# Loads of w_in by even and odd partitions, the first chunk's work regrouped, and two query blocks in buffers of their own

## The chip, the cores and the metric

The kernel runs on one core of a Trainium2 chip. The metric is the time of one execution on the device in microseconds (us). The core has a matrix engine (PE; its weight loads are shown apart as PEld), a vector engine (DVE), a scalar engine (ACT), a general engine (POOL, GpSimd) and a queue engine (SP) that issues most of the loads. SBUF is the on-chip memory of 128 partitions; PSUM is where PE writes, eight banks of 512 float32 a partition.

## The reference

Cosformer attention over 8 batches of 8 heads, 576 positions, head size 64, then a feed-forward layer over all 4608 tokens (512 to 2048 to 512):

```python
r = np.maximum(x, 0.0)                              # x is q or k
phi = np.concatenate([r * c, r * s], axis=-1)       # c, s: cos and sin of the position
kv = np.einsum('bhsf,bhsd->bhfd', k_p, v)
z = np.sum(k_p, axis=2)
num = np.einsum('bhsf,bhfd->bhsd', q_p, kv)
den = np.einsum('bhsf,bhf->bhs', q_p, z)[..., None] + 1e-06
attn = num / den                                    # tokens x 512: head * 64 + d
h = attn @ w_in
out = (h * (1.0 / (1.0 + np.exp(-beta * h)))) @ w_out
```

## The kernel before

**Tiling.** A batch is nine blocks n of 64 query positions. The feed-forward layer takes 512 tokens (eight blocks) at a time; that is a chunk, nine in all, so chunk 0 holds blocks 0 to 7 of batch 0, chunk 1 block 8 of batch 0 and blocks 0 to 6 of batch 1, chunk 2 blocks 7 and 8 of batch 1 and six of batch 2. Blocks 7 and 8 of batch 1 are thus wanted only by chunk 2.

**Attention of one batch.** load_raw (L76) brings q, k and v from DRAM into one buffer each (raw_q, raw_k, raw_v), which the next batch uses again. q_relu and k_relu (L195, L199) clip them into qb and rk (bf16), v_scale (L202) writes v times cosine and v times sine into vb, the first as nine DVE instructions of a block each, the second shared with ACT. q_turn_pe (L227) or q_turn_dma (L258) transposes qb into qt; tan_mul (L222) multiplies that by the tangent into qs. kv_mm (L270) builds kv; num_mm (L290) multiplies qt and qs with it; x_rden and x_mul (L303, L315) divide into xs, one of whose rows is two heads side by side; x_turn_pe or x_turn_dma (L351, L365) transposes xs into xt, the input of the layer. A DMA transpose is issued on SP like a load.

**The layer.** h_mm and h_act (L380, L391) are the first matmul and its activation for one of 16 groups jt of hidden units; o_part and o_mm (L553, L539) the second matmul of chunk 0. From chunk 1 on the second matmul has seven block products instead of eight (o_fast, L556), from chunk 3 on the first as well; these want sums on DVE: g_sum (L397) writes S1 to S4 from the activations, w_sums (L874) T1 to T4 from w_out, wh_sum (L436) those of w_in. In o_fast the product "1" goes to a bank, ACT copies it away ("c1", L602), and "6" adds to that same bank and reads S2; "a7" (DVE, L608) takes the bank before product "4" goes into it.

**Weights.** w_in comes as four stages of 1 MB (load_w, L95), one buffer w_stage each, and is cast to bf16 into win[i] (cast_win, L105); w_out takes the same four buffers after it (cast_out, L117). A stage holds w_in's rows in their order and win[i] holds them with the heads regrouped, so a cast goes in pieces of 64 partitions (GJ, L126).

**Order.** The program is written out by hand, engine by engine in the order of the calls. Up to L746 stands the start with batch 0 and stage 0 of w_in. Then comes a loop of 32 slots (L854): slots 0 to 15 are chunk 0's first matmul, 16 to 23 its second by quarters, 24 to 31 by one jt each for all four token tiles. The dictionary early (L807) hangs batch 1 onto slots: the eighth block of batch 0 and the list rest (L761, casts of w_in, the loads of batch 1 and w_out) after slot 4, kv of batch 1 after slot 22, its query transposes after 23 (second), its num after 25 and 26, x_turn_pe after 28 and 29. Batch 2 is loaded at slot 24 (L868). Then the 16 groups of chunk 1 (L882): num_rest, the last two blocks of batch 1, and att_q(2), the queries of batch 2, stand after group 0, k_all(2) after group 4, w_sums after 6, kv_all(2) and the tan_mul of batch 2 after 10; behind the loop q_relu(3) and the second matmul of chunk 1 (L911). Chunks 2 to 8 follow from lists (L938).

Each DMA issued on SP takes one of eight semaphores in turn and waits for the one eight issues before it.

Of the kernel before, what the change touches and what calls it, by code (L numbers as in the profile page):

```python
# [22 lines left out]
def kernel(  # L23
# [52 lines left out]
    def load_raw(b, name, j0=0, j1=4):  # L76
        js = slice(j0, j1)
        src = {"q": q, "k": k, "v": v}[name][b]
        nc.sync.dma_start(  # L79
            out=raw_tile(b, name)[:, js].rearrange("q j n d -> q j (n d)"),  # L80
            in_=src.rearrange("(j g) (p n) d -> (g p) j (n d)", g=2, n=NQ)[:, js, :])
# [8 lines left out]
    S1, S2, S3, S4 = (const.tile([P, JT // 2, TCH // 2], BF16, name=f"S{i}") for i in (1, 2, 3, 4))  # L90
    w_in_v = moe_w_in.rearrange("(j p) f -> p j f", p=P)
# [3 lines left out]
    def load_w(kind, i, step=4):  # L95
        if (kind, i) not in stages:
            stages[kind, i] = stage.tile([P, 4, 512], FP32, name="w_stage", tag="w_stage")
        st = stages[kind, i]
        for a in range(0, 4, step):
            if kind == "out":  # L100
                nc.sync.dma_start(out=st[:, a : a + step], in_=w_out_v[:, 4 * i + a : 4 * i + a + step, :])
                continue
            nc.sync.dma_start(out=st[:, a : a + step], in_=w_in_v[:, a : a + step, i * 512 : (i + 1) * 512])

    def cast_win(i, gj, eng="dve", f0=0, f1=512, jps=slice(0, 2)):  # L105

        g, jj = gj
        o = win[i].rearrange("q (jp g) f -> q jp g f", g=2)[jj * HP : (jj + 1) * HP, jps, g, f0:f1]
        a = stages["in", i].rearrange("q (jp jj) f -> q jp jj f", jj=2)[g * HP : (g + 1) * HP, jps, jj, f0:f1]
        if eng == "act":  # L110
            nc.scalar.copy(o, a)
        elif eng == "pool":
            nc.gpsimd.tensor_copy(o, a)
        else:
            nc.vector.tensor_copy(o, a)
# [10 lines left out]
    GJ = [(0, 0), (0, 1), (1, 0), (1, 1)]  # L126

    load_raw(0, "q", 0, 2)
    load_raw(0, "q", 2, 4)
    beta16 = const.tile([JT, P], FP32, name="beta16")  # L130
    nc.scalar.dma_start(out=beta16, in_=moe_beta.rearrange("(j p) -> j p", p=P))
# [63 lines left out]
    def q_relu(b, jp, eng="dve", n0=0, n1=NQ):  # L195
        return relu(qb[:, jp, n0:n1].rearrange("q n (j d) -> q j n d", j=2),
                    raw_tile(b, "q")[:, 2 * jp : 2 * jp + 2, n0:n1], eng)

    def k_relu(b, j0=0, j1=4, eng="dve", n0=0, n1=NQ):  # L199
        relu(rk.rearrange("q n j d -> q j n d")[:, j0:j1, n0:n1], raw_tile(b, "k")[:, j0:j1, n0:n1], eng)  # L200

    def v_scale(b, cs, jp=None, n0=0, n1=NQ, eng="dve"):  # L202
        t = (cos9, sin9)[cs]
        rv = raw_tile(b, "v")
        js = slice(0, 4) if jp is None else slice(2 * jp, 2 * jp + 2)
# [21 lines left out]
    def q_turn_pe(b, jp, bank, hold=False):  # L227

        parts = ((0, 0, 5), (1, 5, NQ))
        v2 = []  # L230
        for i, n0, n1 in parts:
            t = ps[:, bank + i].bitcast(BF16)[:, 0 : (n1 - n0) * P].rearrange("q (n c) -> q n c", c=P)
            v2.append(t)
            for n in range(n0, n1):
                nc.tensor.matmul(t[:, n - n0, :], lhsT=qb[:, jp, n, :], rhs=ident,
                                 is_transpose=True, start=(n == n0), stop=(n == n1 - 1))
        def take(e, i):
            _, n0, n1 = parts[i]
            if e == "act":
                nc.scalar.copy(qts[b % 2][:, jp, n0:n1], v2[i])  # L240
            else:
                tan_mul(nc.vector, qs_first[:, jp, n0:n1], v2[i], n0, n1)

        if hold:
            return take
        for e, i in (("act", 0), ("dve", 1), ("act", 1), ("dve", 0)):
            take(e, i)
# [22 lines left out]
    def kv_mm(b, jp, bank, jjs=(0, 1)):  # L270
        t = kv_out(jp, bank)
        for n in range(NQ):
            for jj in jjs:
                for g in range(2):
                    hs = slice(g * HP, (g + 1) * HP)
                    nc.tensor.matmul(  # L276
                        t[jj * HP : (jj + 1) * HP, g], lhsT=rk[hs, n, 2 * jp + jj, :],
                        rhs=vb[hs, n, 2 * jp + jj].rearrange("q s e -> q (s e)"),
# [10 lines left out]

    def num_mm(b, n, jp, bank, slot):  # L290

        for cs in range(2):
            for jj in range(2):
                rows = slice(jj * HP, (jj + 1) * HP)
                for g in range(2):
# [3 lines left out]
                        lhsT=(qts[b % 2], qs_of(b))[cs][rows, jp, n, cols],  # L299
# [15 lines left out]
    def x_mul(got, n0, n1):  # L315
        nv, rden, first, jps = got
        a, z, w = n0 - first, n1 - first, len(jps)
        o = xs[:, n0:n1, jps[0] : jps[-1] + 1].rearrange("q n s (j d) -> q j n s d", j=2)
# [6 lines left out]
    def x_mul_act(got, n):  # L325
        nv, rden, first, jps = got
        for s_, jp in enumerate(jps):
            for jj in range(2):
                nc.scalar.activation(xs[:, n, jp, jj * D : (jj + 1) * D], nv[:, jj, n - first, s_, 0:D],
# [355 lines left out]
    warm_pe(58, 48)  # L685
# [7 lines left out]
    for bank, n0, n1 in ((6, 0, 5), (7, 5, NQ)):  # L693
        nc.vector.tensor_copy(tanr[:, n0:n1, :].rearrange("q n p -> q (n p)"), ps[:, bank, 0 : (n1 - n0) * HP])
# [47 lines left out]
    for gj, eng in zip(GJ, ("pool", "dve", "pool", "dve")):  # L742
        cast_win(0, gj, eng, jps=slice(0, 1))
    for gj, eng in zip(GJ, ("act", "pool", "pool", "pool")):
        cast_win(0, gj, eng, jps=slice(1, 2))
# [10 lines left out]
    def cast_halves(i, fs=(0, 256)):  # L756
        for f in fs:
            for gj in GJ:
                cast_win(i, gj, "pool" if i > 1 and gj == GJ[3] else "dve", f, f + 256)

    cast_halves(1)  # L761

    def rest():

        cast_halves(2)
        cast_halves(3)
        x_mul(x_rden(2, 0, 8, NQ, (0, 1)), 8, NQ)
# [4 lines left out]
        load_raw(1, "q")  # L772
        load_w("out", 2, 2)
        load_w("out", 3, 2)
        x_turn_dma(0, 8, 9)
# [5 lines left out]
        q_relu(1, 0)  # L781
        q_relu(1, 1, n1=5)
# [6 lines left out]
    takes = []  # L789

    def second():

        takes.append(q_turn_pe(1, 0, 4, hold=True))
        takes.append(q_turn_pe(1, 1, 6, hold=True))
        cast_out(8)
        takes[0]("act", 0)
        takes[0]("dve", 1)
        cast_out(9, "a")
        takes[0]("dve", 0)
        takes[0]("act", 1)  # L800
        cast_out(10)
        for e, i in (("act", 0), ("dve", 1), ("act", 1), ("dve", 0)):
            takes[1](e, i)
        for j in (11, 12, 14, 15):
            cast_out(j, "a")

    early = {  # L807
        4: lambda: (num_mm(0, 8, 0, 2, 0), num_mm(0, 8, 1, 2, 1), rest()),
        15: lambda: (v_scale(1, 1, n1=8, eng="act"), k_relu(1, 2, 4, "act")),
        22: lambda: (kv_mm(1, 0, 6), kv_mm(1, 1, 6), kv_take((0, 1), 6, "act"), q_relu(1, 1, "act", 5)),  # L810
        23: second,
        25: lambda: (num_seven(0, 4), x_mul(x_rden(4, 0, 0, 7, (0,)), 0, 7), cast_out(13)),
        26: lambda: (num_seven(1, 6), x_mul(x_rden(6, 0, 0, 7, (1,)), 0, 7)),
        28: lambda: x_turn_pe(1, 0, 7, 4, ("act",), (0,)),
        29: lambda: x_turn_pe(1, 0, 7, 5, ("dve",), (1,)),
    }

    def num_rest():
        for n in range(7, NQ):
            for jp in range(2):  # L820
                num_mm(1, n, jp, 2, 2 * (n - 7) + jp)
        x_mul(x_rden(2, 0, 7, NQ, (0, 1)), 7, NQ)
# [31 lines left out]
    for slot in range(32):  # L854
# [13 lines left out]
        if slot == 24:  # L868
            for name in "qvk":
                load_raw(2, name)  # L870
# [10 lines left out]
    wx_tiles()  # L881
    for slot in range(16):  # L882
        h_group(1, slot)
        if slot == 0:
            num_rest()
# [9 lines left out]
        elif slot == 10:  # L895
            kv_all(2, eng="act")
            for jp in range(2):
                tan_mul(nc.vector, qs_of(2)[:, jp], qts[0][:, jp], 0, NQ)
    q_relu(3, 0, "act")
    q_relu(3, 1, "act")  # L900
    q_turn_dma(3)

# [11 lines left out]
    ops(y, "1 c1")  # L914
    for t, bank in enumerate((4, 6, 0)):
# [176 lines left out]
```

## Time and profile before

| | us |
|---|---|
| three runs: median (lowest to highest) | 274.01 (273.54 to 274.51) |
| the profiled execution: its own time | 274.44 |
| its span in the profile | 272.7 |
| PE busy | 265.3 (97%) |
| DVE busy | 224.0 (82%) |
| ACT busy | 188.4 (69%) |
| POOL busy | 68.3 (25%) |
| mean granted PE clock (1.00 is full) | 0.998 |

PE is busy 3.94 us of the first 5, then 5.00, 3.64 and 4.81 of the next three times 5, all of 20 to 60, 9.18 of 60 to 70, 9.85 of 70 to 80, and all but 0.07 of 80 to 230 (the table of busy time by stretch). Part of the first 17 us is matmuls on zeros that only keep PE running (warm_pe, warm_long).

The chain that ended last is read from the end backwards: at each step it goes to what released that step. A busy share alone says little here; what a step is worth is seen from which of two waits ends later at its place.

### The profile page before, as it was taken

The numbers are of one execution on the slowest core, as the hardware profiler recorded it, in microseconds if no ns is written. First come the engines' busy times: TensorE is split into PE (matmuls) and PEld (weight loads), VectorE is DVE, ScalarE is ACT, GpSimd is POOL, SyncE is SP. The second block draws the span as 40 slices with busy tenths as digits, with TensorE's granted clock in tenths as the row PEclk, the third lists the DMA queues.
The fourth block names the chain that finished last, engine by engine and source line by source line (L and its number), as shares of the span: only waits on it lengthen the run. The fifth ranks groups of instructions, "written<-read, shape, count | busy, mean of one in ns | idle before, by whom it ended". The sixth has DMA issues, their size and how long they took to land.

```text
span 272.7 us, 8970 instructions
## 1 busy us (share of the span) xinstructions
PE 265.3 (97%) x3712; PEld 206.8 (76%) x3712; DVE 224.0 (82%) x596; ACT 188.4 (69%) x384; POOL 68.3 (25%) x89
## 2 busy tenths in 40 slices
PE   8899999999899999999999999999999999999994
PEld 8554455455784588888888888888888888888883
DVE  5989969499989889789989997899589768757852
ACT  4778777796419656899489966996696179428920
POOL 1444000510078000660085009300840060000001
PEclk9999999999999999999999999999999999999999
DMA  6999999999969999994589439943600570015005
GB/s 237 374 395 383 392 390 319 379 201 336 284 130 311 240 348 226 240 313 103 147 216 370 92 58 223 332 71 62 181 2 2 61 185 1 2 27 130 0 2 155
DMA packets 50681, 54.00 MB, mean 198 GB/s; under 512 B 31232, under 2 KB 31760, under 8 KB 50640
## 3 DMA queue, kind: packets, MB, share of 16 engines
q1 hardware_dynamic: 47504, 45.55, 59.1%
q0 software_dynamic: 2784, 7.61, 9.6%
q8 instruction: 29, 0.48, 0.7%
q10 hardware_dynamic: 352, 0.27, 0.4%
q14 instruction: 12, 0.10, 0.1%
HBM read 36.71 MB, written 9.44 MB: 169 GB/s over the span
## 4 chain that ended last, share of the span: by engine, by line
PE 85%; DVE 9%; DMA 3%; SPq 1%; issue 1%; ACT 1%; DVEq 0%
PE ps L621 32%; PE ps L511 27%; PE ps L386 10%; PE ps L544 5%; PE ps L563 4%; PE ps L297 3%; DMA raw_v<-in_v_dram 3%; PE ps L276 3%; DVE vb L219 1%; DVE xs L319 1%; DVE qs L223 1%; SPq L79 1%; DVE S L406 1%; DVE rk L193 1%; DVE qb L193 0%
## 5 line engine op out<-in xcount | busy, mean ns | idle before, releaser
L537 POOL DMA_DIRECT2D out_dram<-o_sb x58 | 33.9, 591 | 147.3 <-ACT o_sb L658 86.3
L420 ACT ACTIVATE g_t<-ps,beta 128x512 bf16<-128x512 f32 x96 | 60.3, 702 | 1.4 <-PE ps L511 1.3
L621 PEld LDWEIGHTS <-S 128*128 128x128 bf16 x448 | 43.4, 98 | 5.2
L511 PE MATMUL ps<-w_stage 128*128 128x256 bf16 x288 | 46.6, 272 | 0.1
L386 PE MATMUL ps<-xt,win 128*128 128x512 bf16 (+1 forms) x196 | 42.8, 375 | 0.1
L511 PEld LDWEIGHTS <-w_stage 128*128 128x128 bf16 x384 | 37.3, 98 | 5.1 <-issue 0.2
L487 DVE TENSOR_TENSOR ps<-ps,p 128x256 f32<-128x256 f32 x74 | 30.5, 428 | 8.6 <-PE ps L511 3.0
L394 ACT ACTIVATE g_t<-ps,beta 128x512 bf16<-128x512 f32 x48 | 32.3, 688 | 7.2 <-PE ps L386 7.1
L621 PEld LDWEIGHTS <-g_t 128*128 128x128 bf16 x336 | 32.3, 98 | 4.5 <-ACT g_t L420 0.4
L386 PEld LDWEIGHTS <-win 128*128 128x128 bf16 x196 | 18.7, 98 | 21.1 <-issue 0.5
L511 PE MATMUL ps<-xt,win 128*128 128x256 bf16 x192 | 32.9, 273 | 0.0
L511 PEld LDWEIGHTS <-win 128*128 128x128 bf16 x288 | 28.0, 98 | 3.4
L621 PE MATMUL ps<-wout,g_t 128*128 128x256 bf16 x224 | 28.9, 273 | 0.0
L406 DVE TENSOR_TENSOR S<-g_t 128x512 bf16<-128x512 bf16 (+1 forms) x66 | 25.7, 418 | 3.3 <-ACT g_t L420 1.7
L480 ACT COPY ps<-ps 128x256 f32<-128x256 f32 x62 | 22.6, 383 | 7.5 <-PE ps L621 4.0
L217 ACT ACTIVATE vb<-raw_v,sin 128x256 bf16<-128x256 f32 (+1 forms) x58 | 26.0, 503 | 1.5 <-DMA raw_v<-in_v_dram 1.5
L621 PE MATMUL ps<-T,S 128*128 128x256 bf16 x224 | 26.6, 273 | 0.0
L621 PE MATMUL ps<-wout,S 128*128 128x256 bf16 x224 | 26.4, 273 | 0.0
L319 DVE TENSOR_TENSOR xs<-ps,rden 128x768 bf16<-128x768 f32 (+4 forms) x26 | 22.8, 884 | 0.9 <-DVE rden L312 0.2
L223 POOL TENSOR_TENSOR qs<-qt,tanr 128x1152 bf16<-128x1152 bf16 x6 | 14.3, 2387 | 27.4 <-PE ps L563 21.0
L658 ACT COPY o_sb<-ps 128x512 f32<-128x512 f32 x11 | 6.3, 587 | 20.1 <-PE ps L621 20.1
L487 DVE TENSOR_TENSOR ps<-ps,u 128x256 f32<-128x256 f32 x36 | 15.3, 427 | 5.3 <-PE ps L511 3.3
(112 smaller groups left out, 414.7 us busy)
## 6 DMA issues: line engine op xcount, KB each, us to landing
raw_v<-in_v_dram SPq DMA_DIRECT2D x7, 1152.0 KB, 9.7
raw_k<-in_k_dram SPq DMA_DIRECT2D x7, 1152.0 KB, 9.5
raw_q<-in_q_dram SPq DMA_DIRECT2D x7, 1152.0 KB, 7.4
out_dram<-o_sb POOLq DMA_DIRECT2D x58, 128.0 KB, 4.5
w_stage<-in_moe_w_in_dram SPq DMA_DIRECT2D x3, 1024.0 KB, 12.8
w_stage<-in_moe_w_out_dram SPq DMA_DIRECT2D x2, 1024.0 KB, 7.9
w_stage<-in_moe_w_out_dram SPq DMA_DIRECT2D x4, 512.0 KB, 11.9
out_dram<-o_sb SPq DMA_DIRECT2D x10, 128.0 KB, 2.4
```

Of the source, the lines that this page charges most:

```text
L217: got = nc.scalar.activation(o, a, AF.Copy, scale=t[:, n : n + 1])
L223: return eng.tensor_tensor(dst.rearrange("q n (g p) -> q n g p", g=2), src.rearrange("q n (g p) -> q n g p", g=2), tanr[:, n0:n1].unsqueez ...
L319: nc.vector.tensor_tensor(o.rearrange("q j n s d -> q j (n s) d"), nv[:, :, a:z, :, 0:D].rearrange("q j n s d -> q j (n s) d"), rden[:, :, ...
L386: nc.tensor.matmul(ps[:, h_bank(c, jt), i * 64 : (i + w) * 64], lhsT=win[jt // 4][:, mi, (jt % 4) * P : (jt % 4 + 1) * P], rhs=xt[:, i : i ...
L394: return nc.scalar.activation(gs[c, jt // 4][:, jt % 4], ps[:, h_bank(c, jt)], AF.Silu, scale=beta[:, jt : jt + 1])
L406: return nc.vector.tensor_tensor(o, l, r, op=op)
L420: return nc.scalar.activation(gs[c, jt // 4][:, jt % 4], bank, AF.Silu, scale=beta[:, jt : jt + 1])
L480: return nc.scalar.copy(at("a", 0), at("b", 0))
L487: nc.vector.tensor_tensor(dst, at("b", 0), st["p5"], op=ALU.add)
L511: nc.tensor.matmul(dst, lhsT=l[:, g], rhs=r[:, :, g * HP : (g + 1) * HP], start=start and g == 0, stop=g == 1, skip_group_check=True)
L537: (eng or own).dma_start(out=out_v[bb, n][:, m0:m1], in_=o_sb[hf * HP : (hf + 1) * HP, m0:m1])
L621: nc.tensor.matmul(dst, lhsT=l(i), rhs=r[:, i], start=start and i == 0, stop=i == order[-1], skip_group_check=True)
```

## The change

- **Heads** of q, k and v are taken in another order (heads), so that a pair jp is j = jp and jp + 2 and not 2jp and 2jp + 1. x_mul writes the two heads of a row of xs element by element in turn, a step of two bf16, and not side by side.
- **w_in** is loaded by two DMAs where there was one, into the even and into the odd partitions; win[i] and its stage then have one layout, and a cast takes all 128 partitions. Stage 0 is cast by POOL, DVE, ACT, POOL (four casts for eight), stages 1 to 3 by four DVE casts each (for eight, two of them on POOL in stages 2 and 3).
- **The start:** a DMA of 16 rows of 32 bytes from v of batch 0 goes out on ACT ahead of beta's (touch), 74 short matmuls on zeros stand at the beginning for 58, and the two copies of tanr move from DVE to ACT.
- **Slots 16 to 31:** num of batch 0's block 8 moves from slot 4 to slot 22 (a copy of its qs is kept in S2), the query transposes of batch 1 from 23 to behind 25, its num behind 27, x_turn_pe behind 30 and 31. The loads of w_out's stages 2 and 3 and of batch 1's queries take turns.
- **Two blocks at home elsewhere:** queries 7 and 8 of batch 1 are loaded into S3 and clipped into S4 (late_raw, late_qb; S1 to S4 are free until chunk 1's sums), transposed by two DMAs on SP, and multiplied by the tangent on POOL. PE transposes 14 blocks of batch 1 and not 18. The loads of batch 2 are issued inside slot 25's list: q, then the DMA transpose of batch 0's block 8, then v, then the two new transposes, then k.
- **Chunk 1:** its first four groups begin with their first two products each; num_rest goes from group 0 to group 10, its x_mul stands behind w_sums on DVE, and q_relu(3) on ACT goes behind the two "c1" copies.

```diff
+    def heads(j0, j1):
+        if j1 - j0 == 4:
+            return slice(0, 4)
+        at = 2 * (j0 % 2) + j0 // 2
+        return slice(at, at + 1) if j1 - j0 == 1 else slice(at, 4, 2)
+    S1, S2, S3, S4 = (const.tile([P, JT // 2, TCH // 2], BF16, name=f"S{i}") for i in (1, 2, 3, 4))
+    late_raw = S3.rearrange("q i t -> q (i t)").bitcast(FP32)[:, 0 : 4 * 2 * D].rearrange("q (j n d) -> q j n d", j=4, n=2)
+    late_qb = S4.rearrange("q i t -> q (i t)")[:, 0 : 2 * 2 * P].rearrange("q (s n c) -> q s n c", s=2, n=2)
...
-    w_in_v = moe_w_in.rearrange("(j p) f -> p j f", p=P)
+    w_in_v = moe_w_in.rearrange("(jj mi d) f -> jj d mi f", jj=2, d=HP)
...
-            nc.sync.dma_start(out=st[:, a : a + step], in_=w_in_v[:, a : a + step, i * 512 : (i + 1) * 512])
+            for jj in range(2):
+                nc.sync.dma_start(out=st[jj:P:2, a : a + step],
+                                  in_=w_in_v[jj, :, a : a + step, i * 512 : (i + 1) * 512])
+    def cast_win(i, mi0, mi1, eng="dve", f0=0, f1=512):
+        o, a = win[i][:, mi0:mi1, f0:f1], stages["in", i][:, mi0:mi1, f0:f1]
...
+    touch = const.tile([2 * H, 8], FP32, name="touch")
+    nc.scalar.dma_start(out=touch, in_=v[0].rearrange("h (s r) d -> (h s) r d", s=2)[:, 0, 0:8])
     nc.scalar.dma_start(out=beta16, in_=moe_beta.rearrange("(j p) -> j p", p=P))
...
-        parts = ((0, 0, 5), (1, 5, NQ))
+        parts = ((0, 0, 5), (1, 5, NQ)) if b == 0 else ((0, 0, 4), (1, 4, 7))
...
-        o = xs[:, n0:n1, jps[0] : jps[-1] + 1].rearrange("q n s (j d) -> q j n s d", j=2)
+        o = xs[:, n0:n1, jps[0] : jps[-1] + 1].rearrange("q n s (d j) -> q j n s d", j=2)
...
-    warm_pe(58, 48)
+    warm_pe(74, 48)
...
-        nc.vector.tensor_copy(tanr[:, n0:n1, :].rearrange("q n p -> q (n p)"), ps[:, bank, 0 : (n1 - n0) * HP])
+        nc.scalar.copy(tanr[:, n0:n1, :].rearrange("q n p -> q (n p)"), ps[:, bank, 0 : (n1 - n0) * HP])
...
-    for gj, eng in zip(GJ, ("pool", "dve", "pool", "dve")):
-        cast_win(0, gj, eng, jps=slice(0, 1))
-    for gj, eng in zip(GJ, ("act", "pool", "pool", "pool")):
-        cast_win(0, gj, eng, jps=slice(1, 2))
+    for mi, eng in enumerate(("pool", "dve", "act", "pool")):
+        cast_win(0, mi, mi + 1, eng)
...
         load_raw(1, "v")
         load_raw(1, "k")
-        load_raw(1, "q")
-        load_w("out", 2, 2)
-        load_w("out", 3, 2)
-        x_turn_dma(0, 8, 9)
+        load_w("out", 2, 2, 0, 2)
+        load_raw(1, "q", n1=7)
+        load_w("out", 2, 2, 2, 4)
+        load_w("out", 3, 2, 0, 2)
+        load_raw(1, "q", n0=7)
+        load_w("out", 3, 2, 2, 4)
...
+    def eighth():
+        for jp in range(2):
+            num_mm(0, 8, jp, 4, jp)
+        kv_mm(1, 0, 6)
+        kv_mm(1, 1, 6)
+        kv_take((0, 1), 6, "act")
+        x_mul(x_rden(4, 0, 8, NQ, (0, 1)), 8, NQ)
...
+    def turn():
+        load_raw(2, "q")
+        x_turn_dma(0, 8, NQ)
+        load_raw(2, "v")
+        takes = [q_turn_pe(1, jp, 4 + 2 * jp, hold=True) for jp in range(2)]
...
+        for jp in range(2):
+            relu(late_qb[:, jp].rearrange("q n (j d) -> q j n d", j=2), late_raw[:, jp::2], "act")
+        for jp in range(2):
+            nc.sync.dma_start(out=qts[1][:, jp, 7:], in_=late_qb[:, jp].rearrange("q n c -> q (n c)"), transpose=True)
+        load_raw(2, "k")
...
+        22: eighth,
+        25: turn,
+        27: sevens,
+        30: lambda: x_turn_pe(1, 0, 7, 4, ("act",), (0,)),
+        31: lambda: (x_turn_pe(1, 0, 7, 5, ("dve",), (1,)), q_rest()),
...
-        if slot == 24:
-            for name in "qvk":
-                load_raw(2, name)
...
+    for jt in range(4):
+        h_mm(1, jt, (0, 1))
     for slot in range(16):
-        h_group(1, slot)
+        if slot < 4:
+            h_mm(1, slot, (2, 3))
+            h_act(1, slot)
+        else:
+            h_group(1, slot)
         if slot == 0:
-            num_rest()
             att_q(2)
...
         elif slot == 10:
+            num_rest()
             kv_all(2, eng="act")
+            x_rest()
...
-    q_relu(3, 0, "act")
-    q_relu(3, 1, "act")
-    q_turn_dma(3)
...
     ops(y, "1 c1")
+    q_relu(3, 0, "act")
+    q_relu(3, 1, "act")
+    q_turn_dma(3)
```

## Prediction, made before the changed kernel ran

> **What bounds the kernel now.** I read the table of busy time by stretch first: PE is busy without a gap from 20 to 60 us and from 80 to 230, so a change in the front can gain only where PE starts its real work, in PE's few waits, and in PE's own work. The chain of waits, in order of time (start, us, what), says what sets the start and the one wait:
>
> ```profile
> 3.16 9.06 DMA raw_v<-in_v_dram
> 12.25 0.92 DVE vb L209
> ...
> 18.65 0.40 PE ps L356 x4
> 19.04 3.03 PE ps L386 x18
> ...
> 51.92 0.18 DVE den L308
> ...
> 66.66 2.02 DVE S L406 x6
> 68.69 1.15 ACT qb L192
> 69.83 0.27 ACT p L602
> 70.15 10.64 PE ps L563 x96
> ```
>
> Up to 18.65 it runs over the second half of raw_v and DVE; from 51.92 to 68.69 over DVE, for 17 us in which PE is full. That means that DVE there is only just in time for PE. The list of waits has PE's one long wait, and DVE's in the same region:
>
> ```profile
> PE ps L563 <- ACT p L602: 1.0, 1, 1.0
> DVE den L308 <- PE ps L297: 2.5, 1, 2.5
> ```
>
> The timelines of ACT and DVE show both. ACT clips batch 3's queries first (after 0.82 us for their landing) and copies p, for which PE waits, only then; DVE idles 2.46 us for num_rest on PE:
>
> ```profile
> 67.62 2.22 ACT L192 ACTIVATE qb<-raw_q 128x1152 bf16<-128x1152 f32 x2 [0.82 <-DMA raw_q<-in_q_dram]
> 69.74 0.63 ACT L602 COPY p<-ps 128x256 f32<-128x256 f32 x2
> 51.92 0.17 DVE L308 TENSOR_TENSOR den<-ps,eps 128x8 f32<-128x8 f32 x1 [2.46 <-PE ps L297]
> 56.67 1.35 DVE L193 TENSOR_SCALAR rk<-raw_k 128x2304 bf16<-128x2304 f32 x1
> ```
>
> The span is 272.7, the execution's own time 274.44: 1.7 us lie around the span, and it is 0.43 above the median of 274.01. I work out a difference and take it from the median.
>
> **The start: +0.06 - 0.07, about 0.** The touch costs ACT an issue like beta's (0.45), so the tangent, ready at 3.42, comes at 3.87. Sixteen more matmuls at 43 ns (2.50 us by 58) add 0.69; PE reaches the tangent's transposes at 4.24, not 3.56, and the query turn at 6.60, not 5.94: +0.66. DVE, busy without a break from there, starts its tan_mul at 7.78. Two things absorb that: the 0.19 us that DVE waits at 12.06 for raw_v's second half, and the k clip at 10.46, which took 0.86 us for 512 elements beside POOL's v_scale (9.14 to 11.04), while 640 elements of q take 0.485 alone. Starting at 11.1 it is alone: 0.45, so 0.41 less. 0.66 - 0.19 - 0.41 = 0.06. The two tanr copies (0.49 and 0.43) go to ACT, which idles from 4.59 to 6.69. After it, one DVE cast goes (1.18 for two, now 0.42), but den waits for PE's num at 16.72 instead of DVE's 16.83: -0.07. Bounds: +0.66 if nothing absorbs; -0.3 if everything is earlier, since PE itself is full to 18.26.
>
> If the touch works, it removes a dip: the DMA moved 405 GB/s from 3 to 5 us, 337 from 5 to 8, and the first half of raw_v landed (8.97) 2.70 us after q's second half, which came 1.43 after its first. That is 0 to 1.27 us of earlier landings. In the start DVE can't use them; behind it they count once, below.
>
> The Trainium skill (SBUF — State Buffer, Who interferes with whom) says that GpSimd and a DVE operation in a two-port mode lock each other out of a shared port for a whole instruction; the trace agrees (DVE casts of 64x512 take 0.42 alone, 0.72 to 0.83 beside POOL's). Without that rule the k clip keeps its 0.86 and the start would be 0.41 later.
>
> **Casts: 0.** DVE's 22 become 13, POOL's nine two: 13 x 0.42 = 5.5 us of DVE for 11.4 (1.18 before 17 us, 10.23 from 19.11 on). All of it lies beside a full PE. w_in's landings (19.1, 21.8, 24.6 for stages 1 to 3) precede PE's need (22.3, 25.7, 29.2) by 3 to 4.6 us. The 64-partition DMAs carry the same rows of 2 KB; I take the same rate, and the other end is a rival.
>
> **x_mul with a step of two: 0.** No row has this step. 128x768 from PSUM takes 0.96 us (1.25 ns an element), a contiguous cast from PSUM (128x520, 0.69) 1.33, so reading sets its pace. The far bound is half speed, 0.96 x 3 a chunk; DVE idles 40 - 35.4 of 40 us in 110 to 150, so 3.1 us a chunk (27.3 us) hide it barely.
>
> **Slots 16 to 31: -0.4.** Four transposes fewer at 59 ns (18 in 1.07) are -0.24; the 0.2 that PE loses between 44.5 and 45.3 waiting for ACT's last copy of qt goes, since two slots now lie before. I followed each wout cast by landing order: w_out's last three halves at 41.2, 42.6 and 44.9, casts done 0.5 to 2 us ahead of their slots. Batch 2's queries do not load earlier: their issue waits for the clip of blocks 0 to 6, which land at about 39.9, so it comes at 41.2, where before it was at 40.40.
>
> What else moves finds cover. POOL's copy into S2 (256 elements) has 15 us. Its two tangent products for the late blocks stand behind the eight stores, which end at 55.55 now, and take 256/1152 of 2.39, so 0.53 each: done at 56.7, while num_rest, which waits for them, comes at about 60. Num_rest's 0.44 and its x_mul only change places; its DMA transpose (53.08, 2.28 us of SP) goes behind batch 3's three loads, which are issued that much earlier, and has until 79 us. Chunk 1's first products need only ACT's copy of xt, at 49.6, and PE gets there at about 50; ACT then starts its activations up to 0.5 us behind PE, with two banks more before PE would wait.
>
> **The wait for p: -0.96.** With q_relu(3) behind "c1" ACT is free at 66.80 and the wait goes. Together PE could be 1.4 us early. What is late next is DVE.
>
> **DVE from 50 to 79: +0.9, which decides.** DVE no longer waits for num_rest: batch 2's queries (landed 47.8) are clipped at 50.6, the nine v instructions end at 54.4. Then it wants raw_k(2), at 54.4 and not at 56.67. That landed at 41.43 + 13.8 = 55.2, and two DMA transposes now stand ahead of it in SP's queue. The table by stretch shows one (block 8 of batch 0, two squares of 128) among loads:
>
> ```profile
> 38.00:42.00 4.00, 4.00 (x99) 2.75 (x100) 2.61 (x5) 2.65 (x5) 0.00 (x0) 1.00 1.07 391
> 42.00:44.00 2.00, 2.00 (x64) 1.06 (x63) 2.00 (x4) 1.46 (x4) 0.00 (x0) 1.00 1.17 226
> 44.00:46.00 2.00, 1.99 (x63) 1.06 (x62) 1.93 (x6) 2.00 (x4) 0.00 (x0) 1.00 0.93 313
> ```
>
> The last column is GB/s. Against 391 the four us lose 0.84 + 0.40 = 1.24 us for 64 KB. Two such cost at most 2.5; at least their bytes, 131 KB at 391 GB/s, 0.34. I take the middle, 1.4, and half of the touch's gain, 0.6: raw_k(2) at 55.2 + 1.4 - 0.6 = 56.0. SP isn't what delays it: the transposes wait for ACT's clips (about 45.4) and raw_k is issued by 48, before raw_v(2) has landed.
>
> From there, by the steps between DVE's starts: k 1.27, v 1.31, w_sums 4.79, the moved x_mul with its den 1.05, tan_mul 2.54, S1 1.34, S2 1.42, together 13.72: S2 ends at 69.7 (69.34 before). From its end to a7's of the second half were 9.62 us, 0.26 of them a wait for PE: 9.36 gives 79.1, and "4" on PE, at 79.75 before, can start at 79.25: **-0.5**. PE alone would be there at 78.35, so the 1.4 shrinks to 0.5. Every us of raw_k(2) moves the end by one, down to the floor of -1.4 at 55.1.
>
> The Trainium skill (Advanced Engine Details and Errata, X-Bar Transpose) says that transpose DMAs are as fast as regular ones. By that raw_k(2) would land at 54.9, below the floor's point: -1.4. The row at 42 to 46 us speaks against it.
>
> Behind 80 us all follows: chunk 2's xt lands at 77.55, two us ahead of its use. Sum: 274.01 - 0.5 = 273.5.
>
> **Rivals.**
> - *Transposes are cheap or the touch pays in full* (273.51 - 0.9 = 272.6): raw_k(2) by 55.1. For it: the transposes stand together and may pay their 1.24 once. Against it: the dip above. Chance 0.31. The rule of the skill is part of this case.
> - *The two transposes hold raw_k(2) back*, the slower side: 2 x 1.24 and no gain from the touch give 57.7, then S2 ends at 71.4, a7 at 80.8: +1.2, 275.2. It is slower than before from 56.5 on, by more than 0.82 from 57.3. For it: both ends of the dip were measured among loads, as here. Against it: ring order leaves SP time. Chance 0.17.
> - *w_in by halves at half rate*: the 10.9 us from 13.7 to 24.6 become 21.8, stage 3 lands at 35.5, PE needs it at 29.2: about +7, 281. It decides from 10.9/15, 73% of the rate. Against it: even partitions spread over the whole range. Chance 0.03. The Trainium skill (DMA: Bandwidth & Descriptors, Rules for kernel authors) advises one transfer of 128 partitions over two to halves; no row here has two.
> - *x_mul at half speed*: more than 3 us of DVE's reserve used, about +2. Chance 0.04.
> - *The forecast*, raw_k(2) between 55.6 and 57.3: 0.45.
>
> **Chances.** A measurement of this kernel tells about 0.3% (0.82 us) from no change. Faster by more: 0.32; within: 0.45; slower: 0.23. The range goes from the floor with the start's best, 274.01 - 1.4 - 0.3 = 272.3, to the late raw_k(2), 275.2; it leaves out half rate, half speed and a little at both ends, some 0.15.
>
> **What would show it.** Right: no wait of PE L563 for ACT's p; DVE idle at about 54.4 with raw_k as its releaser, for about 1.6 us; raw_k(2) landing at 56; S2's end at 69.7; PE's L356 for chunk 0 at 18.6; the first k clip at 0.45. Wrong: DVE not waiting for raw_k (then -1.4), PE waiting on S2 or a7 (then slower), w_in landing after 25 us, x_mul over 0.96, or PE gaps between 32 and 52 us, where I found none.

## The result, and the profile after

The changed kernel takes 277.04 us (median of six runs, 276.33 to 277.76), the kernel before 273.95 beside it: ratio 1.0112, 95% interval 1.0091 to 1.0133, so 3.1 us slower. The profiled execution took 277.76, the most of the six; its span is 276.0. A second profile of the kernel before, taken later (f1 below), has an own time of 273.49, close to the median of its ten runs (273.63), and one wait of PE less than the first. Of the experiments below, one run of f4 (280.62) and two of g3 (278.91 and 279.80) were slow executions and are left out of their medians. Starts on PE (us) in the three profiles:

| first matmul of | before, first | before, second | after |
|---|---|---|---|
| chunk 0's h behind x_turn | 18.88 | 18.38 | 18.57 |
| slot 16 | 31.77 | 31.26 | 31.79 |
| chunk 1's h | 50.36 | 50.32 | 49.72 |
| kv of batch 2 | 60.44 | 60.40 | 60.07 |
| product "1" | 65.91 | 65.87 | 67.05 |
| product "6" | 70.15 | 69.18 | 71.24 |
| chunk 2's h | 80.62 | 79.66 | 82.49 |
| the last product | 268.71 | 267.77 | 270.94 |

PE is 0.6 ahead of the second profile at chunk 1 and 2.8 behind it at chunk 2: the loss comes between 60 and 82 us. PE's timeline there shows, as the longest of five short waits for DVE, three that the kernel before does not have, and "4" at 81.62, 1.87 later than in the first profile and 2.84 later than in the second (78.78):

```profile
67.05 1.91 PE L577 MATMUL ps<-wout,g_t 128*128 128x256 bf16 x16 [0.52 <-DVE xs L333]
...
69.56 0.23 PE L310 MATMUL ps<-kv,qs 64*64 64x65 bf16 x4 [0.38 <-DVE qs L234]
...
71.24 2.27 PE L577 MATMUL ps<-T,S 128*128 128x256 bf16 x16 [0.35 <-DVE S L420]
...
81.62 1.03 PE L577 MATMUL ps<-T,g_t 128*128 128x256 bf16 x8
```

The first of these is for a bank: num_rest writes bank 2 in group 10 now, and "1" must wait until x_mul has read it. DVE's timeline says why DVE is late. It waits for batch 2's v, then its nine v instructions take 4.26 us, and then it waits for k. In the kernel before the same nine took 2.44, and k began at 56.67 (before's timeline, the first line here):

```profile
54.30 2.44 DVE L219 TENSOR_SCALAR vb<-raw_v,cos 128x256 bf16<-128x256 f32 x9
```

```profile
53.23 4.26 DVE L230 TENSOR_SCALAR vb<-raw_v,cos 128x256 bf16<-128x256 f32 x9 [1.36 <-DMA raw_v<-in_v_dram]
58.39 1.36 DVE L203 TENSOR_SCALAR rk<-raw_k 128x2304 bf16<-128x2304 f32 x1 [0.90 <-DMA raw_k<-in_k_dram]
...
70.76 1.43 DVE L420 TENSOR_TENSOR S<-S,g_t 128x512 bf16<-128x512 bf16 x4
```

The chain of waits goes through the issue of the two late transposes (SPq L832) into raw_k. The table by stretch shows two dips among the loads, at 46 to 48 us (where block 8 of batch 0 is transposed; it landed at 48.7) and at 52 to 54 (the pair, landed at 53.6 and 53.9). The last column is GB/s:

```profile
47.00 0.36 SPq L832
47.36 0.05 issue
47.41 10.96 DMA raw_k<-in_k_dram
58.37 0.02 issue
58.39 1.36 DVE rk L203
```

```profile
46.00:48.00 2.00, 2.00 (x10) 0.90 (x10) 1.93 (x4) 0.99 (x2) 0.00 (x0) 1.00 1.14 136
48.00:50.00 2.00, 2.00 (x22) 1.34 (x20) 0.37 (x2) 1.34 (x3) 0.00 (x0) 1.00 0.95 328
50.00:52.00 2.00, 2.00 (x11) 0.92 (x10) 1.88 (x3) 1.53 (x4) 1.64 (x3) 1.00 2.03 292
52.00:54.00 2.00, 2.00 (x11) 0.88 (x9) 0.77 (x3) 1.92 (x4) 2.00 (x4) 1.00 0.54 146
```

A second kind of loss stands at 19.39 in the chain: PE stops, and nothing that the profile shows releases it ("issue").

```profile
18.73 0.65 PE ps L400 x4
19.39 0.51 issue
19.90 12.05 PE ps L400 x58
```

### The profile page after: what moved, and what is told of

Read it like the earlier page. It is cut to its first block, busy times and chain, and to the rows that moved or that the text cites. A ratio compares the mean times of both kernels' runs of the same rounds, so it can differ in the third digit from the quotient of the medians.

```text
span 276.0 us, 8996 instructions
## 1 busy us (share of the span) xinstructions
PE 264.6 (96%) x3721; PEld 205.7 (75%) x3724; DVE 220.2 (80%) x585; ACT 189.1 (69%) x388; POOL 64.7 (23%) x85
## 4 chain that ended last, share of the span: by engine, by line
PE 81%; DMA 7%; DVE 7%; issue 2%; ACT 1%; SPq 1%; DVEq 0%
PE ps L635 31%; PE ps L525 27%; PE ps L400 10%; DMA raw_k<-in_k_dram 4%; PE ps L577 3%; DMA raw_v<-in_v_dram 3%; PE ps L558 3%; PE ps L310 3%; PE ps L287 3%; DVE qs L234 2%; DVE S L420 1%; DVE xs L333 1%; SPq L91 1%; ACT wout L131 1%; DVE rk L203 1%
## 5 line engine op out<-in xcount | busy, mean ns | idle before, releaser
L400 PEld LDWEIGHTS <-win 128*128 128x128 bf16 x196 | 18.8, 98 | 21.9 <-issue 0.8
L333 DVE TENSOR_TENSOR xs<-ps,rden 128x768 bf16<-128x768 f32 (+4 forms) x26 | 24.3, 942 | 0.8
L230 DVE TENSOR_SCALAR vb<-raw_v,cos 128x256 bf16<-128x256 f32 x63 | 22.4, 405 | 2.7 <-DMA raw_v<-in_v_dram 2.7
L234 POOL TENSOR_TENSOR qs<-qt,tanr 128x1152 bf16<-128x1152 bf16 (+1 forms) x8 | 15.8, 1978 | 29.7 <-DVE den L322 22.9
```

The costliest lines, as they stand in the source:

```text
L230: got = nc.vector.tensor_scalar(o, a, scalar1=t[:, n : n + 1], scalar2=None, op0=ALU.mult)
L333: nc.vector.tensor_tensor(o.rearrange("q j n s d -> q j (n s) d"), nv[:, :, a:z, :, 0:D].rearrange("q j n s d -> q j (n s) d"), rden[:, :, ...
L400: nc.tensor.matmul(ps[:, h_bank(c, jt), i * 64 : (i + w) * 64], lhsT=win[jt // 4][:, mi, (jt % 4) * P : (jt % 4 + 1) * P], rhs=xt[:, i : i ...
```

## The experiments

Each result is given as the median time in us and its ratio to the kernel before on the same chip, with the 95% interval of the ratio.

### The late transposes and DVE's chain

**e1_k_ahead**

```diff
         load_raw(2, "v")
+        load_raw(2, "k")
...
-        load_raw(2, "k")
         cast_out(12)
```

> The changed kernel, with raw_k of batch 2 issued straight behind its raw_v, ahead of the two late DMA transposes. Theory A (the two late transposes in SP's queue hold raw_k(2) back; DVE's chain behind it makes PE wait at the w_out products): raw_k(2) lands at about 56.0 and not 58.4, DVE's second S sum ends at about 69.8 and not 72.2, PE's waits there (0.52 for xs, 0.38 for qs, 0.7 for S, about 0.8 at kv) go, 277.0 - 2.4 = 274.6. Rival B (DVE's own additions behind raw_k, the moved x_mul first of all, and x_mul's slower step): raw_k's landing does not decide, 276.4 to 277.2. Rival C (the late transposes, now behind raw_k, land at about 58.5, POOL's two products end at 59.6 and num_rest waits at about 60): a new wait of PE of 0.5 or more ahead of num_rest, 275 to 276.

277.27, 1.0159 (1.0129 to 1.0189): no gain. raw_k landed at 56.3, near what was expected, but S2 ended at 70.9 and not at 69.8. The pair of transposes, now behind raw_k, lets POOL's tangent products start only at 56.6. The nine v instructions ahead of k then took 2.45 us as in the kernel before, and the five behind k, now beside POOL's products, took 2.24 and not 1.40.

```profile
56.28 1.36 DVE L203 TENSOR_SCALAR rk<-raw_k 128x2304 bf16<-128x2304 f32 x1 [1.01 <-DMA raw_k<-in_k_dram]
57.56 2.24 DVE L230 TENSOR_SCALAR vb<-raw_v,sin 128x256 bf16<-128x256 f32 x5
```

Then chunk 2's first product waited for its own xt (x_mul at 78.30, transpose landed at 82.01, PE 82.06). Moving a load ahead moved the lateness on. The number lies just above B's range; the way to it is no theory's.

**e2_no_late_turn**

```diff
-            nc.sync.dma_start(out=qts[1][:, jp, 7:], in_=..., transpose=True)
+            nc.scalar.copy(qts[1][:, jp, 7:], late_qb[:, jp])
```

> The changed kernel, with the two late DMA transposes left out: ACT copies the late blocks' clipped queries, not transposed, into the place of the transposed ones (two copies of 128x256 more on ACT, about 0.35 each), so that those two query blocks are not the reference's. Theory A: raw_k(2) lands 2.0 to 2.4 us earlier, at 56.0 to 56.4, PE's waits between 60 and 73 go, 274.6. Rival B (what DVE does behind raw_k costs it): 276.4 to 277.2 although raw_k lands early. Rival D (the dip in the queue is block 8's transpose, not the late ones): raw_k lands at 58 still, 277.

275.12, 1.0060 (1.0045 to 1.0075): by the ratios 1.4 of the 3.1 us are gone; A's time (274.6) was missed by half a us. raw_k landed at 56.3 as A says, but DVE took it only at 57.22, because its nine v instructions took 4.33 us. POOL's products stand beside them here, and four of the nine took 0.75 to 0.85 us each, not 0.35:

```profile
52.97 4.33 DVE L230 TENSOR_SCALAR vb<-raw_v,cos 128x256 bf16<-128x256 f32 x9 [0.65 <-DMA raw_v<-in_v_dram]
57.22 1.35 DVE L203 TENSOR_SCALAR rk<-raw_k 128x2304 bf16<-128x2304 f32 x1
55.52 1.37 POOL L234 TENSOR_TENSOR qs<-qt,tanr 128x256 bf16<-128x256 bf16 x2
```

The profile tells POOL's spans only roughly: the slow four run from 54.0 to 57.0. That the slow instructions go where POOL's products go is seen from e1. S2 ended at 71.0, PE still lost 0.75 between "6" and chunk 2, and chunk 2 began at 81.29, 1.6 behind the second profile of before. That is all of the 1.6 us that e2 has left.

**f4_sums_first**

```diff
             att_q(2)
+            w_sums()
             v_half(2, 0)
...
-        elif slot == 6:
-            w_sums()
-        elif slot == 10:
+        elif slot == 12:
             num_rest()
```

> The changed kernel, with DVE's four sums of w_out taken at slot 0 of chunk 1, ahead of batch 2's v and k, and num_rest, kv and x_rest at slot 12 and not 10. Theory A (DVE's chain behind raw_k(2) is what PE waits for): DVE sums from 51.9 to 56.7 where it idled, clips k at about 59.1, ends v at 61.7 and S2 at about 68, not 72.2, though raw_k lands no earlier; PE's waits between 60 and 73 go, chunk 2 starts at 80.2 to 80.5: 274.8. Rival B (PE waits for other things there too, the bank that x_rest reads for one): chunk 2 at 81.5 or later, 276 or more.

276.76, 1.0092 (1.0060 to 1.0123). DVE ran as in the second profile of before from S1 to 78 us (within 0.15), and chunk 2 started at 80.49 as theory A expected, 2.0 earlier than in the changed kernel. Yet the time did not follow (A: 274.8). A short wait for chunk 2's xt, 1.28 us at 109.3 (PE waits for DVE, and DVE waited 1.49 for a raw_v that was issued at 97.6, not 94.0) and the end, 1.0 longer than in the second profile of before, took most of it back. That DVE's chain behind raw_k sets this stretch holds; that it is all of the loss does not.

**g4_before_two_turns** and **h4_before_two_turns_c1** (the second with e3's edit as well)

```diff
-            for name in "qvk":
+            for name in "qv":
                 load_raw(2, name)
+            for i in range(2):
+                nc.sync.dma_start(out=S4..., in_=zeros[:, 0 : 2 * P], transpose=True)
+            load_raw(2, "k")
```

> The kernel before, with two DMA transposes of 128x256 zeros (into a tile that is free) ahead of raw_k(2) in SP's queue: the disputed cost by itself. By the two measured costs in the changed kernel (2.0 for the pair): raw_k(2) lands at 57.2 to 57.9 where it landed at 55.2 to 55.9, DVE clips k 0.6 to 1.2 later than at 56.67, S2 ends as much later, and PE, which had at most 0.2 us to spare there, with it: 274.2 to 274.9. By the prediction's middle (1.4 for the pair): raw_k(2) at 56.6 to 57.3, 273.6 to 274.2. If transposes are as fast as other DMAs (0.34 for their 131 KB): raw_k(2) at 55.6 to 56.2, no change.

g4: 275.30, 1.0055 (1.0037 to 1.0072), above all three forecasts. The price of the pair alone: raw_k(2) landed at 56.8 in g4 and in h4, where seven profiles with before's order have 55.3 to 56.2 (mean 55.75), so 1.0. DVE's k began only 0.15 later. The time went another way: the loads behind were later too, batch 3's q landed at 68.4, and ACT clipped it ahead of p, for which PE waited 1.8 us.

```profile
68.48 2.22 ACT L192 ACTIVATE qb<-raw_q 128x1152 bf16<-128x1152 f32 x2 [1.70 <-DVE S L406]
70.60 0.62 ACT L602 COPY p<-ps 128x256 f32<-128x256 f32 x2
```

> The kernel before, with the two DMA transposes of zeros ahead of raw_k(2) and ACT's clips of batch 3's queries behind the two c1 copies. Theory (with the two transposes alone raw_q(3) landed at 68.4, ACT clipped it at 68.5 to 70.6 ahead of p, and PE waited 1.8 us for p; DVE's chain was only 0.15 later): the wait for p goes, 273.6 to 274.1. Rival (the pair costs by DVE's chain): 274.8 to 275.4, as without the move.

h4: 274.65, 1.0032 (1.0020 to 1.0045), between the two forecasts. In the profile the wait for p is gone, and that execution took 273.82, as expected, but it is the fastest of the ten. Their median keeps 0.9 us over before; from what, the one profile does not show.

### The wait for p

**f1_before_again**: no edit. **e3_before_c1**:

```diff
-    q_relu(3, 0, "act")
-    q_relu(3, 1, "act")
-    q_turn_dma(3)
...
     ops(y, "1 c1")
+    q_relu(3, 0, "act")
+    q_relu(3, 1, "act")
+    q_turn_dma(3)
```

> The kernel before, unchanged, for a second profile of it on the chip of the runs beside it. If the first profile of it stands for its usual execution: span 272.7, own time 274.4, chunk 2's first h product on PE at 80.6, a wait for p of about 1.0 ahead of it. If the first profile was a slow execution (the median is 0.4 to 1.0 below its own time): span 271.6 to 271.9, and the place where it is shorter shows what the other profiles are to be compared with.

> The kernel before, with only ACT's clips of batch 3's queries and their DMA transpose moved behind the two c1 copies. Theory A (the wait for p was worth what DVE leaves: PE could go on 0.96 earlier, but S2 ends only 0.2 after PE is ready): 0.65 to 0.8 less, 273.2. Rival E (DVE bounds this stretch already, or batch 3's queries are then late): 273.8 to 274.4.

f1: 273.63, span 271.7. e3: 273.67, 1.0001 (0.9986 to 1.0016). PE's starts in the profile of e3 are those of the second profile of before ("6" at 69.32, chunk 2 at 79.81), and f1 shows the reason: the wait for p is not there to be removed. Batch 3's q landed at 65.5 in f1 and not at 67.5, so ACT clipped it as soon as it was free and came to p 0.97 earlier:

```profile
66.66 2.21 ACT L192 ACTIVATE qb<-raw_q 128x1152 bf16<-128x1152 f32 x2
68.77 0.64 ACT L602 COPY p<-ps 128x256 f32<-128x256 f32 x2
```

### w_in and x_mul

**e4_before_w_in**: before with heads, w_in_v, load_w, cast_win, the casts and the step in x_mul of the change, nothing else.

> The kernel before, with only w_in in even and odd partitions (its two loads a stage, casts over 128 partitions, x_mul with a step of two, head order). Theory A (as forecast, these cost nothing): 273.7 to 274.3. Rival F (x_mul's step costs: 0.94 us on the mean and not 0.88, three of them in DVE's chain from 67 to 73 us, and 0.5 us of PE's pause at 19.4 to 19.9 comes with the new casts): 274.6 to 275.0.

275.41, 1.0074 (1.0048 to 1.0100), above both forecasts. Its profile shows one wait of PE behind 20 us that the second profile of before does not have, a pause in the row of short num products:

```profile
67.61 1.12 PE ps L302 x112
68.73 1.15 issue
69.88 0.41 PE ps L302 x26
```

Stage 3 of w_in landed at 24.7 (24.5 and 24.6 in the two profiles of before, 24.8 in after). The 18 instructions of x_mul over 768 elements took 1.022 us each on the mean, not 0.958, in after, and 1.023 in e4. So the landings are as theory A says, and its time is not.

### PE's instruction loads

A record is one executed instruction in the trace; PE's are its products and its weight loads together. The page of the profile counts the loads of program code among the DMA queues (after; number, MB, share of the engines):

```profile
q8 instruction: 29, 0.48, 0.8%
```

29 loads of 16 KB for about 7,450 records of PE are about 64 bytes a record, so a load holds about 256 records. Counted in records, the pauses with "issue" of 0.16 us and more in all profiles (17 of them, without a kind of 0.16 at 38.9 to 39.8 us, 13 us and more behind the last load) stand at 706, 1216, 1983 or 1986, 4541 or 4542, and 5310 or 5313. Each is 189 to 194 more than a multiple of 256, whatever the kernel, and in each PE goes on 1.2 to 1.6 us after a load's packets end (h1: load from 42.1 to 43.2, PE at 44.5; e4: 67.4 to 68.5, PE at 69.9; f3: 70.1 to 71.2, PE at 72.5). That PE waits for its code there is read from these places and times; no run changed the load itself.

**f3_warm58** (`warm_pe(74, 48)` to `warm_pe(58, 48)` in the changed kernel), **h3_after_warm62** (to 62), **h1_before_warm74** (before with 74), **g3_before_start** (before with the touch, 74 and ACT's tanr copies), **h2_before_touch** (g3 with 58):

> The changed kernel, with 58 warming products and not 74. Theory G (PE's pause at 19.4, 0.51 long, is a block boundary of PE's code that falls where the next block has not landed): 32 instructions fewer move it behind longer products, the pause goes or moves, and h of slot 4 comes 0.5 earlier, but the end moves only as far as DVE's chain behind raw_k lets it: 276.5 to 277.0. Rival I (the pause is a wait for ACT's copy of xt): the pause stays. Theory of the prediction (the 16 products cost nothing at the end): 277.0.

> The kernel before, with only the start changed (the touch, 74 warming products, tanr copied by ACT). The prediction's term (0.06 - 0.07): 273.4 to 273.9, the same as before. Rival (the touch brings raw_v's second half and with it the start 0.3 earlier): 273.1 to 273.3. Rival G (32 more instructions on PE move a block boundary of its code into a row of short products): 274.3 or more, with a pause of PE at a place where the recorded instructions are 192 more than a multiple of 256.

> The kernel before, with 74 warming products and not 58: 32 instructions of PE more and nothing else. Theory G (the start costs 1.8 because 32 instructions move the block boundaries of PE's code, and PE pauses where the next block has not landed): as the whole start did, 275.0 to 275.6, with pauses of 0.5 or more at recorded instruction 1216, 1984 or 4541 or another that is 192 more than a multiple of 256. Theory of the prediction (0.66 at the most, if nothing absorbs 16 products): 273.6 to 274.2, with a later query turn and no pause.

> The kernel before, with the touch and with ACT copying tanr, but with the 58 warming products: the start without its 32 PE instructions. Theory G: 273.3 to 273.8, the same as before, no pause of PE at a block boundary. Rival (the touch or ACT's copies cost the start): 274.3 or more, and then chunk 0's first h product 0.3 or more later.

> The changed kernel, with 62 warming products, by which PE has as many instructions as the kernel before. Theory G (the same boundaries as before from chunk 2 on): the pauses at 19.4 and at 157 go, 276.0 to 276.6, if none comes in their place among the short products at 68 to 71 us; with one there 277 to 278.5. DVE's chain behind raw_k keeps chunk 2's first product at 81.5 or later in either case.

| | us | ratio | pauses of PE with "issue" over 0.3 |
|---|---|---|---|
| f3 | 279.93 | 1.0210 (1.0167 to 1.0253) | 2.62 ending at 72.5, 0.64 at 185.0 |
| g3 | 275.12 | 1.0065 (1.0039 to 1.0092) | 0.75 at 44.5, 0.64 at 155.2 |
| h1 | 275.85 | 1.0064 (1.0039 to 1.0089) | 0.66 at 44.5, 0.49 at 156.6 |
| h2 | 273.76 | 1.0006 (0.9992 to 1.0020) | none |
| h3 | 277.25 | 1.0120 (1.0097 to 1.0143) | 1.02 at 71.0, 0.62 at 181.7 |

g3, h2 and h3 came out as theory G says, h1 a little above it (275.0 to 275.6); f3 missed every forecast. h1 and h2 part the start cleanly: its 32 more instructions cost all of it, the touch and ACT's copies nothing. It is not the later start that costs: at slot 16 h1 (32.26) and h2 (32.19) are level, and at chunk 1, behind h1's pause at 44.5, h1 is 0.9 later. h1 also shows how a pause can grow. Chunk 1 is 1.0 later than in before, batch 3's q lands at 69.0, and the wait for p appears (the list of PE's waits). In g3, as late at chunk 1, q landed at 67.0 and no such wait came.

```profile
PE ps L563 <- ACT p L602: 1.4, 1, 1.4
...
PE ps L297 <- issue: 0.7, 1, 0.7
PE ps L621 <- issue: 0.5, 1, 0.5
```

f3 took the pause at 19.4 away and got one of 2.62 for it. In its table by stretch the seventh column is the granted clock, which fell to 0.50 after PE had stood still. Changing the count moves the pauses and does no more: h3, with before's count, is no faster than the changed kernel.

```profile
68.00:70.00 2.00, 1.51 (x124) 1.19 (x122) 2.00 (x6) 1.79 (x3) 0.00 (x0) 1.00 1.05 391
70.00:72.00 2.00, 0.00 (x0) 0.00 (x0) 1.93 (x8) 0.70 (x1) 0.00 (x0) 1.00 1.32 141
...
74.00:76.00 2.00, 2.00 (x11) 1.45 (x10) 1.93 (x6) 0.37 (x1) 0.00 (x0) 0.50 0.99 170
```

### The end, and all together

**f2_sp_pad** (14 small loads more on SP in chunk 6), **g1_dve_pad** (eight settings of one column on DVE there), **g2_all_mended** (f4 with kv at slot 13, g1's settings, 62 warming products):

> The changed kernel, with 14 loads of 16 words each added on SP in chunk 6, where SP is idle for tens of microseconds; nothing reads them. Theory G (the end of the changed kernel, where SP stands still from 272.44 to 274.66 beside an instruction load of 8 KB at 272.9, is a block boundary of SP's own code that falls between its last waits; before, the like load came at 267.3, beside the last products): the boundary moves away from the end, the last wait ends about 1.0 earlier, 276.0, and the span from DVE's last operation to the end is 3.7 and not 4.7. Rival H (the last stores themselves land later): no change at the end, 277.0.

> The changed kernel, with eight settings of one column each added on DVE in chunk 6; nothing reads them. Theory G2 (the 8 KB instruction load at 272.9, beside the last stores, is DVE's own: it starts as DVE reaches its 704th instruction of the record in every profile, at 266.1 before and 272.9 after, since DVE has fewer instructions now): the load comes at 265 to 270 again, from DVE's last operation to the end of the span takes 3.7 us and not 4.7, 276.0. Rival H (the end is longer for another reason, the last stores): 277.0, whatever the load does.

> The changed kernel with the found causes taken out together: DVE's sums of w_out at slot 0 of chunk 1, num_rest at slot 12 and kv at slot 13, the eight settings on DVE, and 62 warming products, with which PE has as many instructions as before. Theory (DVE's chain behind raw_k, PE's instruction loads and the load at the end are all that the change costs; what it gains in slots 16 to 31, 1.1 us against the second profile of before, stays): no wait of PE over 0.2 between 60 and 80, chunk 2's first product at 79.5 to 80.2 (79.7 in the second profile of before), 273.3 to 274.3. Rival (something else in the change costs, x_mul or the loads): 275 or more, without such waits.

f2: 277.38, 1.0128 (1.0106 to 1.0150); the load stayed at 272.4, so it isn't SP's. g1: 276.74, 1.0115 (1.0092 to 1.0138); the load moved to 267.2 and DVE's last operation stood 3.6 us ahead of the end and not 4.3, but the median shows nothing of that. The load is DVE's. In the six profiles in which it runs beside the last stores (from 272.0 to 275.8 on), 3.9 to 4.4 us lie behind DVE's last operation; in the twelve others, where it comes earlier or only after the end, 3.2 to 3.6. What that is worth in the median stays below what these runs tell. g2: 275.77, 1.0099 (1.0067 to 1.0132), above its forecast. DVE kept PE waiting nowhere behind 18 us, but a pause of 1.20 with "issue" ended at 69.9, at record 1983. No version was faster than the kernel before.

## Why the prediction was wrong, point by point

The forecast was 273.5, the measured time 277.04. The slower rival had the right mechanism: its landing of raw_k(2), 57.7, is close to the mean of the profiles with this order (57.9). Its price (275.2) was too small, because it was counted from the first profile of before.

- **"DVE from 50 to 79", the failing step.** It let DVE end the nine v instructions at 54.4 and take raw_k(2) at 56.0. DVE ended them at 57.5 and took raw_k at 58.39. Both halves failed.
  - *The landing.* raw_k(2) landed at 58.4, and at 57.5 to 58.4 in the seven profiles with this order. The sum was 55.2 + 1.4 - 0.6. The pair's 1.4 was fair: 1.0 alone (g4, h4), 1.2 to 2.1 in the changed kernel (against e2). The start of the sum was not: the profile that it was read from is the earliest of seven (mean 55.75). The touch's 0.6 was nothing: with it and before's loads raw_k(2) landed at 56.2 and 55.5 (h2, g3), and raw_v's first half at 8.6 and 9.0, as in the profiles without it (8.3 to 9.0). Another 0.5 over the mean stands even without the pair ahead of raw_k (56.3 in e1 and e2); from what, the runs do not show. It is not that block 8's transpose moved, since in the kernel before it also stood ahead of raw_k(2), issued at 34.3 and landed at 44.8.
  - *DVE's v.* POOL's two products for the late blocks were counted as POOL's time only. Beside them the nine v instructions took 4.3 us and not 2.4, as e2 shows (e1, with the products later, has 2.45). They begin when raw_v(2) has landed, at 53.2 in after and 52.9 in e2; even from 52.33, its landing in the first profile of before, 2.44 us give 54.8 and not 54.4. So a raw_k at 56.0 would have been taken only at about 57.2, as in e2. The Trainium skill (SBUF — State Buffer, Who interferes with whom) says that GpSimd and a DVE operation in a two-port mode block each other on a shared port for a whole instruction. The trace agrees (0.75 to 0.85 us for 0.35), and the forecast, which cites the rule for the k clip, did not apply it here.
  - *The chain behind it held.* 58.39 + 13.72 = 72.11, and S2 ended at 72.19; by 9.36 more a7 at 81.55, and "4" began on PE at 81.62. In five profiles with this order of DVE's work (after, e2, f2, g1, h3) DVE's k began at 58.39, 57.22, 57.60, 58.34 and 57.77, and chunk 2 on PE at 82.49, 81.29, 81.69, 82.42 and 81.88, each time 24.1 later. So every us by which k is late moves chunk 2 by one, as forecast. Only f3, with its pause of 2.62, and e1, which waits for xt, are later than that.
- **The wait for p: -0.96.** It is gone in after, but that is worth nothing (e3). It was an event of the one profiled execution, whose own time stood 0.43 above the median; I took it for a property of the kernel. In these profiles it goes with the landing of batch 3's q: none at 65.5 (f1), 0.96 at 67.5, 1.8 at 68.4 (g4). The -0.5 of the sum was counted from that profile too, with "4" at 79.75. The second profile has it at 78.78, so even a "4" at 79.25 would have been 0.5 later and not 0.5 earlier.
- **The Trainium skill on DMA transposes** (Advanced Engine Details and Errata, X-Bar Transpose) has them as fast as regular DMAs. The measurement decides against it here: 131 KB cost raw_k(2) 1.0 us by themselves (g4, h4), and their bytes are 0.34 at 391 GB/s.
- **The start: about 0.** The sum held: chunk 0's h behind x_turn began at 18.4 to 18.9 in six profiles without the change of the start and at 18.5 to 18.9 in the nine of the changed kernel and its variants. With the start's change alone it began at 18.8 and 19.3 (g3, h2), and h2 is at 1.0006. In part the sum held by luck. The k clip's 0.41 is no gain of the change: the second profile of before has the clip at 0.42 without it, since POOL's v_scale began at 8.46 there and at 9.14 in the first. What was not on the list costs 1.8 by the ratio in the kernel before: 32 more PE instructions (h1), with which PE pauses where it did not before.
- **Casts, w_in at half rate.** The landings are about as before, and the rival of half rate did not come. The Trainium skill (DMA: Bandwidth & Descriptors, Rules for kernel authors) advises one transfer of 128 partitions over two of halves; here two made the last landing 0.4 later at the most (24.9 for 24.5). e4's 2.0 us show as a pause at record 1986 with the same number of PE instructions as before; why that load came late is open.
- **x_mul with a step of two: 0.** It costs 0.06 an instruction, 24.3 us for 22.8 in all. Three of them stand in DVE's chain from 66 to 76 us: at most 0.2.
- **Slots 16 to 31: -0.4.** From slot 16 to chunk 1's first product seven profiles of before's order took 18.2 to 19.1 (mean 18.6; g3 and h1 with their pauses left out), nine of the changed kernel and its variants 17.9 to 18.5 (mean 18.1): -0.5. PE cannot use it, because it then waits for DVE.

How it adds up. Chunk 2 starts 2.8 later in after than in the second profile of before: 1.8 because DVE's k begins at 58.39 and not at 56.62, and 1.05 for the moved x_mul with its den, which now stands in the chain behind it. Without the pair k is 1.2 earlier, chunk 2 is 1.2 earlier, and the ratio falls by 1.4 us (e2). Behind chunk 2 the profile of after loses 0.32 in a pause with "issue" and 1.1 between DVE's last operation and the end, in all 4.3 us more than the second profile of before; it is the slowest of six executions, and the medians differ by 3.1. The pause of 0.51 at 19.4 is not part of this: f2 has only 0.12 of it, and its chunk 2 stands as far behind k. What stays open is why f4 and g2, which relieve DVE's chain, gain so little. Their profiles show other losses in its place, and w_in alone (e4) and 32 PE instructions alone (h1) cost the kernel before 2.0 and 1.8, so the parts cannot be added.

## What to carry over

Before a wait is priced, it has to be shown to be in the usual execution. An own time above the median says that the profile may hold a wait that usually isn't there, and a landing read from one profile has a spread (0.9 us here) that belongs into the sum. Work that is moved to another engine has to be priced on its neighbours too, here POOL's products on DVE's v. A transfer put ahead of a load was paid here by the loads behind it as well, and it showed where the next of them was just in time, with p. In a kernel that keeps PE full, a few instructions more on it can cost more than the time that they take, so a control with the same instruction count belongs beside each edit.

## What the runs showed of the hardware, unexpected

PE's code comes in by DMA, 16 KB for about 256 instructions. In a row of short products (112 of 64x65 in 1.12 us in e4's chain, each with its weight load) a block lasts some 1.3 us, by estimate. Most loads take about 1.1 and PE goes on 1.2 to 1.6 after it, so where a load starts late PE stands still, in these profiles for up to 2.6 us. What delays a load is not shown. After the longest pause, 2.62 us in f3, the granted clock was at 0.50 for 3.4 us.

DVE's code comes in blocks of 8 KB. Its last load starts at DVE's 703rd to 705th record in all profiles, so a few instructions fewer (706 records for 710) moved it from 266 or 267 us in the two profiles of before to 272.9, beside the last stores.

The trace records PE's full clock from 4.0 to 10.8 us on, in the two profiles of before from 9.0 and 9.6. In the changed kernel and its variants the query turn on PE began at 5.8 in the three profiles with a full clock before 5 us (after, e2, g1) and at 6.4 in the six others, and chunk 0's h behind x_turn at 18.5 to 18.9 in all nine.
